# Clearing expert output columns later on GpSimd, and loading two float64 pieces later

## The chip, the cores and the metric

The kernel runs on one core of a Trainium2 chip. The metric is device microseconds of one execution; the kernel before takes 333.71 us, the median of three runs (333.45 to 333.76).

## The reference, cut to what matters

Three layers run one after the other on 1536 tokens of width 384.

```python
y = _attn_ref(r, k, v, w, u)                 # linear attention with a decaying state: 2 x 768 tokens, 8 heads of 48
logits = x @ w_gate                          # mixture of 8 experts, each token to its best one
# each expert takes its first `capacity` = 384 tokens; the others' output is zero
h = np.maximum(np.einsum('ecd,edf->ecf', disp, w1), 0.0)
out[i] = gate_w[i] * y[expert_idx[i], pos[i]]
h = x @ w_in; e = np.exp(h - h_max); sm = e / (e.sum() + 1e-9)      # SoLU block, w_in and w_out are float64
ln = (h * sm - mu) / np.sqrt(var + 1e-06) * g_ln
return (ln @ w_out).astype(np.float32)
```

## The kernel before, in words

**Attention** walks over 12 blocks of 128 tokens (`for m in range(NM - 1)`, then block 11 by itself). Each block ends as a tile of gated tokens that SP stores to DRAM (`store`, L481). GpSimd scatters the block's tokens' numbers into a table of slots (`scatter`, L486), SP loads a part of that table into `ids` (`load_ids`, L86), and GpSimd gathers an expert's tokens from DRAM with it, two indirect DMAs per expert (`load_xe`, L94). For expert 0 the tokens of the last blocks are not gathered but placed by matmuls with one-hot tiles (`add`, L654). Each of those needs a block's tokens split in a high and a low part; the low part of blocks 8 and 9 is a difference on GpSimd (L575), that of blocks 10 and 11 one on VectorE (L579).

**Experts.** One loop over g from 0 to 33 does a quarter of an expert's hidden layer per step, e being g // 4 and q being g % 4. `mm1(g)` (L822) makes a quarter of the hidden layer, ScalarE and VectorE evict it in a high and a low part (`hh` L828, `hl` L829), and `mm2(g - 2)` (L808 to L810) adds the quarter that was made two steps earlier into the output. The weights come as raw halves by SP (`load_half`, L107) and are split in high and low parts by ScalarE (L116) and VectorE (L122); in some steps GpSimd forms the low part with an adding DMA (L120). `xe_split` (L801 to L804) transposes the next expert's gathered tokens and splits them (`xlo`, L804). After the last quarter an expert's output is evicted to `yT` at a column known only at run time (L859 ScalarE, L860 VectorE); an expert writes 224 columns, of which the next expert's output overwrites the unused ones.

**Clearing.** `yT` is four tiles (high and low part, two shapes). At q == 0 of expert e GpSimd clears the 224 columns that start at (e + 1) * 224, in four memsets (L929), for e from 0 to 6. The first two sets of four run together, eight memsets behind the gather of expert 1.

**Pieces.** w_in and w_out are float64. Each comes as 8 pieces of 384 KB (`load_piece`, L140, on SP, three buffers) and is turned into high and low parts in the loop by ScalarE (L878, L879, L904) and VectorE (`decode_piece`, L887 to L906). Beside a piece's decoding runs one step of `later`, a chain of small VectorE operations on the experts' counts (`starts`, L738 to L754).

After the loop the SoLU block runs over 12 blocks of tokens, TensorE first (`h2`, L1016).

All engines take their instructions in the order in which the program gives them (the schedule is written by hand), and so does each queue: SP's holds the stores, table loads, pieces and raw halves, GpSimd's the scatters, gathers, adding DMAs, inverse positions (`inverse`, L787) and memsets.

Of the kernel before, what the change touches and what calls it, by code (L numbers as in the profile page):

```python
# [8 lines left out]
F32 = mybir.dt.float32  # L9
# [10 lines left out]
N, DM, NE, DF = B * S, H * D, 8, 1024  # L20
C = 128
NM = N // C
# [3 lines left out]
W = 224  # L26
# [9 lines left out]
def rwkv_moe_solu_kernel(  # L36
# [21 lines left out]
    YW = N + max(W, 128 * NOV)  # L58
# [10 lines left out]
    V, S, G, T = nc.vector, nc.scalar, nc.gpsimd, nc.tensor  # L69
# [18 lines left out]
    def load_xe(e, c0, nb, rows=N + 1, t=None):  # L88
        if t is None:
            t = xe_p.tile([128, nb, DM], F32, tag="xe", name=f"xe{e}_{c0}", bufs=1)  # L90
        for b in range(nb):
            c = c0 + b
            n = BW[c] if c < 2 else 128
            nc.gpsimd.indirect_dma_start(  # L94
                out=t[0:n, b, :], out_offset=None, in_=xs[0:rows, :],
                in_offset=bass.IndirectOffsetOnAxis(ap=ids[0:n, e, c:c + 1], axis=0), bounds_check=rows - 1, oob_is_err=False,
            )
        return t
# [37 lines left out]
    def load_piece(p, eng=nc.sync):  # L136
        t = w64_p.tile([128, 384, 2], I32, tag="w64", name=f"w64_{p}")
        s = (w_in if p < NP else w_out).rearrange("p a f -> p (a f)").bitcast(I32)
        j = p % NP
        eng.dma_start(out=t.rearrange("p n c -> p (n c)"), in_=s[:, j * 768:(j + 1) * 768])  # L140
        pieces[p] = t

    def attention(actx):
# [145 lines left out]
        def scores(m):  # L289
            A = a2.tile([128, 2, HP, C], F32, tag="A", name=f"A{m}")  # L290
            kt, rt = kts.pop(m), rts[m]
            both = ps_s.tile([128, 2, HP, C], F32, tag="s", name=f"sp{m}")
            sps = [both[:, r] for r in range(2)]
            for p in range(HP):
                for r in range(2):
                    ps = slice(64 * r, 64 * r + 64)
                    T.matmul(
                        sps[r][:, p], kt[ps, p, :], rt[ps, p, :], start=p == 0, stop=p == HP - 1, skip_group_check=True
                    )
            As[m] = (A, both)  # L300
# [12 lines left out]
        def values(m):  # L313
            yps = ypss[m] = [ps_y.tile([128, 2, C], F32, tag="y", name=f"yp{m}_{q}") for q in range(2)]
            for j in range(HP):
                va = vab[m % 3][:, j].rearrange("p b d -> p (b d)")[:, 0:112]
                T.matmul(
                    yps[j // 2][0:112, j % 2], va, ident, is_transpose=True, start=j % 2 == 0, stop=False,
                    skip_group_check=True,
                )  # L320
# [159 lines left out]
        def store(m):  # L480
            nc.sync.dma_start(out=xs[1 + m * C:1 + (m + 1) * C, :], in_=xgs[m])  # L481
# [3 lines left out]
        def scatter(m):  # L485
            ins = G.indirect_dma_start(  # L486
                out=idx[:, :], out_offset=bass.IndirectOffsetOnAxis(ap=slots.pop(m)[:, 0:1], axis=0),
                in_=row[:, m], in_offset=None, bounds_check=NX - 1, oob_is_err=False,
            )
            for other in scattered:  # L490
                tc.declare_no_dep(ins.ins, other.ins, reason="every token has its own slot")
            scattered.append(ins)
# [92 lines left out]
        for m in range(NM - 1):  # L585
            values(m)
            if m:
                if m + 1 < NM:
                    scores(m + 1)
                if m + 2 < NM:  # L590
                    prelude(m + 2)
                if m + 1 < NM:
                    mask_scores(m + 1)
            attend(m, lambda: ranks(m - 1) if m else None)
            if m == NM - 2:
                state(m)
            if m:
                together(gate2(m - 1))
            if m == NM - LAST + 1:
                xe0 = load_xe(0, 0, 2, 1 + (NM - LAST) * C, ld.tile([128, 3, DM], F32, tag="krv", name="xe0"))  # L600
            if m:
                scatter(m - 1)
            if m < NM - 2:
                state(m)
            while pend:
                pend.pop()()
            if m in first:
                pend.append(split_q(*first[m], False, defer=True))
            if m + 2 < NM:
                products = prelude2(m + 2)  # L610
                next(products)
            if m < NM - 2:
                decay(m + 1)
            tokens(m)
            if m + 2 < NM:
                together(gate1(m), products)
                weigh(m + 2)
                prelude3(m + 2)
            else:
                values(m + 1)  # L620
                attend(m + 1, lambda: None)
                together(gate1(m))
            if NM - LAST < m:
                if m < NM - 2:
                    onehots[m - 1] = place(m - 1)
                his[m - 1] = part(m - 1)
                los[m - 1] = other(m - 1, his[m - 1])
            chunks.pop(m)
            if m + 4 < NM:
                load_chunk(m + 4)  # L630
            if m:
                store(m - 1)
            if m in halves:
                load_half(*halves[m])
            if m == NM - LAST:
                load_ids(0, 1)
            if m == NM - 2:
                load_piece(0)


        m = NM - 1
# [27 lines left out]
        together(steps)  # L669
        scatter(m - 1)  # L670
        store(m - 1)
        load_piece(1)
        ranks(m)
        steps = gate2(m)
        next(steps), next(steps)
# [6 lines left out]
        whole(m)  # L682
        together(steps)
        store(m)
        scatter(m)
        load_ids(1, 2)
        spare(1, fill)
# [21 lines left out]
    def experts_and_solu():  # L709
# [9 lines left out]
        yT = [[ytp.tile([128, n, YW], F32R, name=f"yT{x}{n}") for n in (2, 1)] for x in ("hi", "lo")]  # L719
# [203 lines left out]
        load_half(1, 3)  # L923
        for g in range(NQ + 2):
            e, q = divmod(g, 4)
            if q == 0 and (e + 1) * W < YW:
                for n in range(2):
                    for x in range(2):
                        G.memset(yT[x][n][:, :, (e + 1) * W:min((e + 2) * W, YW)].bitcast(F32), 0.0)  # L929
            if g == 4:  # L930
                mm2(2)
                xe_split(1, xraw)
                xraw = load_xe(2, 0, 2)
                mm2(3)
            tokens = e and q == 2 and e + 1 < NE
            if g < NQ:
                mm1(g)
            if g == NQ + 1:
                mm2(NQ - 1, NQ - 2)
            elif g >= 2 and g not in (4, 5, NQ):  # L940
                mm2(g - 2)
            if g + 3 < NQ:
                split_q(1, g + 3, False)
            if g == 0:
                split_q(2, 2, False)
            if 2 <= g < NQ - 1:
                split_q(2, g + 1, g > 4 and g % 4 == 1)
            if tokens:
                xe_split(e + 1, xraw)
            if tokens and e + 2 < NE:  # L950
                xraw = load_xe(e + 2, 0, 2)
            if g % 2 and g // 2 + 2 < 2 * NP:
                load_piece(g // 2 + 2)
            if g % 2 == 0:
                j = g // 2
                if g and j + 3 < NQ // 2:
                    load_half(1, j + 3)
                if g and j + 2 < NQ // 2:
                    load_half(2, j + 2)
            if g == 0:  # L960
                load_ids(2, NE)
            if g in (8, 26):
                for _ in later:
                    pass
            if g == 16:
                later = positions()
            if NQ - 5 <= g < NQ - 1:
                for m in range(3 * (g - NQ + 5), 3 * (g - NQ + 6)):
                    inverse(m)
            if g == NQ - 2 and NOV:  # L970
                tc.no_sync_barrier()
                tc.mark_branch_hint_location("over", "LikelyTaken", [ENG.PE, ENG.Activation, ENG.DVE, ENG.Pool, ENG.SP])
            if g == 20 and NOV:
                most.append(nc.values_load(
                    mxi[0:1, 0:1], min_val=0, max_val=N, skip_runtime_bounds_check_because="a count of tokens",
                ))
            if dec:
                decode()
            if g % 2 and g < 4 * NP - 1:
                dec = decode_piece(g // 2)  # L980
                decode()
            if g % 2 == 0 and g // 2 < 2 * NP:
                decode_early(g // 2)
# [246 lines left out]
```

## Time and profile before

| | |
|---|---|
| runs | 333.71 us median (333.45 to 333.76) |
| profiled execution | 332.55 us, of which the span from first to last instruction is 330.8 us |
| TensorE busy | 315.5 us (95%) |
| VectorE busy | 242.7 us (73%) |
| ScalarE busy | 187.2 us (57%) |
| GpSimd busy | 148.0 us (45%) |

Attention takes about 76 us, the experts go on to about 212 us, and the SoLU block fills the rest. Busy shares are means over stages: what a change in one of them is worth is read from the waits in that stage. A timeline line has the start, the length, the engine, the line, the operation with its tiles and shapes, and, in brackets, how long the engine sat idle before it and what ended that.

### The profile page before, as it was taken

The page shows a single profiled execution, that of the slowest core. Times are in us where ns is not written, and L with a number is a line of the kernel's source. Part 1 is how long each engine was busy: PE and PEld are TensorE (multiplying, and loading weights), DVE is VectorE, ACT ScalarE, POOL GpSimd, SP SyncE. Part 2 cuts the span into 40 slices and gives each one's busy share as a digit, 9 for nine tenths or more (in the row PEclk, how much of TensorE's full clock was granted, in tenths as well). Part 3 has the DMA queues.
Part 4 walks back from the last instruction along what each step waited for, and adds up shares of the span by engine and source line. Part 5 has one row for each costly group of instructions (what it writes and reads, how often), then busy time and mean ns, then how long its engine had stood idle before and what let it go on. Part 6 is the DMA issues. An engine that isn't in the chain of part 4 may idle for free. (4 is left out here: it accounts for less than half of the span.)

```text
span 330.8 us, 7363 instructions
## 1 busy us (share of the span) xinstructions
PE 315.5 (95%) x2747; PEld 289.9 (88%) x2747; DVE 242.7 (73%) x557; ACT 187.2 (57%) x406; POOL 148.0 (45%) x197
## 2 busy tenths in 40 slices
PE   8899989999989999999999999999999999999990
PEld 3688868879979999999999999978999999999990
DVE  7899999958989999898999896258745555434310
ACT  2545645649549796969696966126454433444410
POOL 7989899572523241423232454414254222333321
PEclk9999999999999999999999999999999999999997
DMA  6999999353778998989898913100000000000010
GB/s 207 399 335 274 368 400 381 120 147 116 237 276 257 297 297 295 287 283 275 279 283 292 273 60 49 11 0 2 2 24 29 21 24 24 26 24 24 26 48 24
DMA packets 20394, 56.23 MB, mean 170 GB/s; under 512 B 6594, under 2 KB 9028, under 8 KB 20356
## 3 DMA queue, kind: packets, MB, share of 16 engines
q1 hardware_dynamic: 16916, 47.67, 41.0%
q0 software_dynamic: 3440, 8.06, 10.3%
q8 instruction: 22, 0.36, 0.4%
q14 instruction: 16, 0.13, 0.1%
HBM read 50.56 MB, written 5.16 MB: 168 GB/s over the span
## 5 line engine op out<-in xcount | busy, mean ns | idle before, releaser
L809 PE MATMUL yps<-hl,whi 128*128 128x224 f32 x192 | 52.9, 276 | 0.5 <-DVE hl L829 0.5
L122 DVE TENSOR_TENSOR wlo<-raw,whi 128x768 fp32r<-128x768 f32 x57 | 52.3, 952 | 1.2 <-ACT whi L116 0.9
L808 PE MATMUL yps<-hh,whi 128*128 128x224 f32 x192 | 52.7, 275 | 0.0
L810 PE MATMUL yps<-hh,wlo 128*128 128x224 f32 x192 | 52.5, 273 | 0.0
L116 ACT ACTIVATE whi<-raw 128x768 fp32r<-128x768 f32 x64 | 50.6, 840 | 0.3 <-ACT hh L828 0.3
L1050 POOL TENSOR_SCALAR e<-e,nmu 128x1024 f32<-128x1024 f32 x12 | 13.5, 1128 | 62.6 <-DVE nmu L1049 59.5
L1027 DVE TENSOR_REDUCE nm<-h 128x1 f32<-128x1024 f32 (+1 forms) x13 | 14.7, 1139 | 33.2 <-PE h L1016 30.0
L809 PEld LDWEIGHTS yps<-hl,whi 128*128 128x128 f32 x192 | 36.9, 192 | 0.7 <-DVE hl L829 0.7
L810 PEld LDWEIGHTS yps<-hh,wlo 128*128 128x128 f32 x192 | 36.9, 192 | 0.0
L808 PEld LDWEIGHTS yps<-hh,whi 128*128 128x128 f32 x192 | 36.9, 192 | 0.0
L120 POOL DMA_DIRECT2D wlo<-in_w x7 | 6.9, 986 | 66.2 <-ACT wlo L125 66.2
L1084 PE MATMUL o<-w_hi,shi 128*128 128x384 f32 x96 | 33.1, 345 | 0.0
L1085 PE MATMUL o<-w_lo,shi 128*128 128x384 f32 x96 | 32.2, 335 | 0.0
L1086 PE MATMUL o<-w_hi,slo 128*128 128x384 f32 x96 | 32.2, 335 | 0.0
L94 POOL DMA_INDIRECT xe<-xs,ids x16 | 20.3, 1270 | 20.6 <-PE xt L801 8.6
L822 PE MATMUL hps<-xlo,whi 128*128 128x224 f32 x192 | 26.8, 275 | 1.5 <-DVE xlo L804 1.5
L822 PE MATMUL hps<-xhi,whi 128*128 128x224 f32 x192 | 27.1, 277 | 0.1
L828 ACT ACTIVATE hh<-hps 128x448 fp32r<-128x448 f32 x32 | 17.4, 543 | 17.1 <-PE hps L822 16.5
L822 PE MATMUL hps<-xhi,wlo 128*128 128x224 f32 x192 | 26.6, 274 | 0.0
L822 PEld LDWEIGHTS hps<-xlo,whi 128*128 128x128 f32 x192 | 24.0, 192 | 1.7 <-DVE xlo L804 1.7
L822 PEld LDWEIGHTS hps<-xhi,whi 128*128 128x128 f32 x192 | 24.0, 192 | 0.6 <-ACT xhi L696 0.6
L822 PEld LDWEIGHTS hps<-xhi,wlo 128*128 128x128 f32 x192 | 24.0, 192 | 0.0
(186 smaller groups left out, 787.7 us busy)
## 6 DMA issues: line engine op xcount, KB each, us to landing
raw<-in_w SPq DMA_DIRECT2D x32, 768.0 KB, 7.2
krv<-in_krv SPq DMA_DIRECT2D x11, 576.0 KB, 6.8
rkT<-in_rkT SPq DMA_DIRECT2D x12, 512.0 KB, 7.6
w<-in_w_in SPq DMA_DIRECT2D x8, 384.0 KB, 5.2
w<-in_w_out SPq DMA_DIRECT2D x8, 384.0 KB, 5.6
wlo<-in_w POOLq DMA_DIRECT2D x7, 384.0 KB, 5.5
xs<-xg SPq DMA_DIRECT2D x12, 192.0 KB, 4.8
krv<-in_krv SPq DMA_DIRECT2D x1, 384.0 KB
```

Of the source, the lines that this page charges most:

```text
L94: nc.gpsimd.indirect_dma_start(out=t[0:n, b, :], out_offset=None, in_=xs[0:rows, :], in_offset=bass.IndirectOffsetOnAxis(ap=ids[0:n, e, c: ...
L116: S.activation(hi, raw, AF.Copy)
L122: V.tensor_tensor(lo, raw, hi.bitcast(F32), ALU.subtract)
L808: T.matmul(ps, w[0][ws], x[0][xsl], start=first, stop=False, skip_group_check=True)
L809: T.matmul(ps, w[0][ws], x[1][xsl], start=False, stop=False, skip_group_check=True)
L810: T.matmul(ps, w[1][ws], x[0][xsl], start=False, stop=last, skip_group_check=True)
L822: T.matmul(ps[:, f], w1s[g][i][:, kk, wf], x[j][:, kk], start=not (i or j or f or kk), stop=j == 1 and kk == KD - 1, skip_group_check=True,)
L828: S.activation(hh, ps, AF.Relu)
L1027: V.tensor_reduce(nms[j], ps, AX.X, ALU.max, negate=True)
L1084: T.matmul(ps, hi[:, f % 4], wo[0][:, f], start=f == 0, stop=False)
L1085: T.matmul(ps, hi[:, f % 4], wo[1][:, f], start=False, stop=False)
L1086: T.matmul(ps, lo[:, f % 4], wo[0][:, f], start=False, stop=f == KF - 1)
```

## The change

At attention's end, pieces 0 and 1 of w_in are loaded later: piece 0 after the store of block 10 instead of one block sooner, piece 1 after the store of block 11 instead of after that of block 10, and so in front of the table load for expert 1.

In the experts' loop the memsets at q == 0 go. Instead, at q == 2 of expert e (1 to 6), behind the issue of the gather for expert e + 2, GpSimd clears the 224 columns that start at e * 224, the ones in which expert e's output, three steps later, can land; the last set stops at column 1536. That makes 24 memsets in place of 28, and none in the first six steps of the loop.

```diff
--- before.py
+++ after.py
@@ -634,8 +634,6 @@
                 load_half(*halves[m])
             if m == NM - LAST:
                 load_ids(0, 1)
-            if m == NM - 2:
-                load_piece(0)
 
 
         m = NM - 1
@@ -669,7 +667,7 @@
         together(steps)
         scatter(m - 1)
         store(m - 1)
-        load_piece(1)
+        load_piece(0)
         ranks(m)
         steps = gate2(m)
         next(steps), next(steps)
@@ -682,6 +680,7 @@
         whole(m)
         together(steps)
         store(m)
+        load_piece(1)
         scatter(m)
         load_ids(1, 2)
         spare(1, fill)
@@ -923,10 +922,6 @@
         load_half(1, 3)
         for g in range(NQ + 2):
             e, q = divmod(g, 4)
-            if q == 0 and (e + 1) * W < YW:
-                for n in range(2):
-                    for x in range(2):
-                        G.memset(yT[x][n][:, :, (e + 1) * W:min((e + 2) * W, YW)].bitcast(F32), 0.0)
             if g == 4:
                 mm2(2)
                 xe_split(1, xraw)
@@ -949,6 +944,10 @@
                 xe_split(e + 1, xraw)
             if tokens and e + 2 < NE:
                 xraw = load_xe(e + 2, 0, 2)
+            if q == 2 and 0 < e < NE and e * W < N:
+                for n in range(2):
+                    for x in range(2):
+                        G.memset(yT[x][n][:, :, e * W:min((e + 1) * W, N)].bitcast(F32), 0.0)
             if g % 2 and g // 2 + 2 < 2 * NP:
                 load_piece(g // 2 + 2)
             if g % 2 == 0:
```

## Rows read from the trace of the kernel before

**Rows 1.** Busy time by stretch: length, PE, PEld, DVE, ACT, POOL, clock, DMA.

```profile
112.00:150.00 38.00, 38.00 (x344) 38.00 (x343) 35.06 (x60) 29.05 (x53) 10.19 (x14) 1.00 0.90 293
```

**Rows 2.** Waits of PE in the whole span: total, times, longest.

```profile
PE hps L822 <- DVE xlo L804: 1.5, 1, 1.5
...
PE x L661 <- DMA xe<-xs,ids: 0.6, 1, 0.6
...
PE yps L809 <- DVE hl L829: 0.5, 1, 0.5
```

**Rows 3.** Timeline of PE around the waits: start, length, line, operation.

```profile
88.38 0.27 PE L808 MATMUL yps<-hh,whi 128*128 128x224 f32 x1
...
89.13 0.37 PE L809 MATMUL yps<-hl,whi 128*128 128x224 f32 x1 [0.48 <-DVE hl L829]
...
91.12 0.74 PE L801 MATMUL xt<-ident,xe 128*128 128x128 f32 x6
...
93.73 0.83 PE L822 MATMUL hps<-xhi,whi 128*128 128x224 f32 x6
...
94.40 0.83 PE L822 MATMUL hps<-xhi,wlo 128*128 128x224 f32 x6
...
96.77 0.93 PE L822 MATMUL hps<-xlo,whi 128*128 128x224 f32 x6 [1.54 <-DVE xlo L804]
```

**Rows 4.** Timeline of DVE in the same stretch.

```profile
84.51 2.75 DVE L740 TENSOR_SCALAR cnt<-tot 128x8 f32<-128x8 f32 x1
...
88.46 0.61 DVE L829 SCALAR_TENSOR_TENSOR hl<-hps,hh 128x448 fp32r<-128x448 f32 x1
...
95.81 0.91 DVE L804 TENSOR_TENSOR xlo<-xt,xhi 128x384 fp32r<-128x384 f32 x2
```

**Rows 5.** Timeline of POOL: gather of expert 1, first and last of eight memsets.

```profile
81.81 1.37 POOL L94 DMA_INDIRECT xe<-xs,ids  x1 [5.48 <-DMA ids<-idx]
...
83.49 1.09 POOL L94 DMA_INDIRECT xe<-xs,ids  x1 [0.31 <-issue]
...
84.59 0.49 POOL L929 MEMSET yThi<- 128x448 f32 x1
...
86.92 0.30 POOL L929 MEMSET yTlo<- 128x224 f32 x1
```

**Rows 6.** Groups by shape on DVE: a tensor_scalar like L740, undisturbed.

```profile
L742 DVE TENSOR_SCALAR cnt<-cnt 128x8 f32<-128x8 f32 x1 | 0.2, 165 | 0.0
```

**Rows 7.** Timelines of POOL and DVE: a later burst's last memset, the decoding after it.

```profile
125.39 0.30 POOL L929 MEMSET yTlo<- 128x224 f32 x1
...
127.08 0.36 DVE L887 TENSOR_SCALAR da<-w 128x384 int32<-128x384 int32 x1
```

**Rows 8.** Timeline of POOL where the added memsets fall: the adding DMAs.

```profile
186.07 0.98 POOL L120 DMA_DIRECT2D wlo<-in_w  x1 [10.30 <-ACT wlo L125]
...
201.96 0.97 POOL L120 DMA_DIRECT2D wlo<-in_w  x1 [5.64 <-ACT wlo L125]
```

**Rows 9.** Timelines of POOL and PE at attention's end: block 9's difference, its matmuls.

```profile
70.76 1.04 POOL L575 TENSOR_TENSOR xl<-xg,xh 128x384 fp32r<-128x384 f32 x1
...
72.28 0.50 PE L654 MATMUL x<-P,xl 128*128 128x224 f32 x3
```

**Rows 10.** Timeline of SP at attention's end: DMA issues.

```profile
72.61 0.42 SPq L140 DMA_DIRECT2D w<-in_w_in  x1
...
75.35 0.32 SPq L481 DMA_DIRECT2D xs<-xg  x1
...
77.49 0.79 SPq L86 DMA_DIRECT2D ids<-idx  x2
```

**Rows 11.** The piece issued at 72.61, from issue to landing.

```profile
DMA to landing us min/median/max: 3.5/3.5/3.5
```

**Rows 12.** Timeline of ACT: the first reader of piece 0.

```profile
80.57 0.57 ACT L878 ACTIVATE w<-w 128x384 int32<-128x384 uint32 x1
```

**Rows 13.** The two gathers of expert 1, from issue to landing.

```profile
DMA to landing us min/median/max: 6.8/6.9/7.1
```


## The prediction

> **What bounds the kernel now.** I read the page first, then the busy time by stretch, the waits of each engine, and the timelines around the waits that were left. In the experts' loop TensorE never stops: from 112 to 150 us it is busy for 38.00 of 38.00, with VectorE next at 35.06 [rows 1]. So an edit there is worth only what it takes from or adds to TensorE's idle time, and the list of its waits is short: once 1.5 us for `xlo`, 0.6 for expert 0's gathered tokens, 0.5 for `hl` [rows 2]. The reader is to see that the first and the last lie within eight microseconds of each other, at 89.13 and 96.77 [rows 3], and that both are waits for VectorE.
>
> VectorE is late there because of one event. At 84.51 a tensor_scalar on 8 columns (L740) starts and takes 2.75 us, while its like (L742) takes 0.165 [rows 6]; it ends at 87.26 [rows 4]. On GpSimd the first of eight memsets starts at 84.59 and the last ends at 86.92 + 0.30 = 87.22 [rows 5]. A VectorE instruction was held for as long as GpSimd cleared columns, and everything behind it, `hl` at 88.46 and `xlo` at 95.81 [rows 4], came that much later.
>
> **The memsets.** Undisturbed, L740 would have ended at 84.51 + 0.165 = 84.68; it ended at 87.26, so VectorE lost 2.58 us. All eight memsets leave this place. What TensorE gets back is worked out from starts. A group of six matmuls of 224 columns takes 0.67 us, from 93.73 to 94.40, so one takes 0.11, and after 88.38 the next was due at 88.49 and came at 89.13: 0.64 lost. After the group at 94.40 the next was due at 95.07 and came at 96.77: 1.70 lost [rows 3]. Together 2.34; the waits that the profile itself puts down, 0.48 + 1.54 = 2.02, are the lower bound.
>
> Is all of it given back? With VectorE 2.58 earlier, `hl` ends at 88.46 + 0.61 - 2.58 = 86.49, two microseconds ahead of need. `xlo` is two instructions in a row that end near 96.72, and would end at 94.14; TensorE, itself 0.64 earlier, wants it at 95.07 - 0.64 = 94.43. That is 0.29 to spare, so nothing is late next on VectorE, and I take 2.34. If the slack were used up, the term shrinks by what is missing, not to nothing.
>
> Behind that point no engine has to give the time back: TensorE has no gap to swallow it [rows 1], weight loads are issued when VectorE frees their buffers, and so move with it.
>
> **The memsets that remain.** The sets for experts 1 to 5 stay where they run now. Today each set, though written two steps later, runs straight behind a gather, since GpSimd has nothing in between. They now must wait for the output of the expert before, which is written one step before the set in the program; behind a set that waits stand the next adding DMA and gather, which wait for ScalarE and TensorE anyway. The 24 waits I cost at nothing. One set is new at this place, that of expert 6, behind the adding DMA at 186.07. Eight memsets took 2.63 us [rows 5], so four take 1.3 (an estimate). Behind them stand twelve inverse scatters, the second half of which starts only after the DMA at 201.96, in front of which GpSimd idles 5.64 us [rows 8]; that idle time hides it. Nothing, then; at worst the 1.3 us falls on VectorE again.
>
> The Trainium skill's page "SBUF — State Buffer", section "SBUF: two separate sides", says that GpSimd and a VectorE instruction in a two-port mode exclude each other from a shared pair of ports, and that the second blocks until the first instruction is through. The trace agrees that VectorE is blocked; it differs on how long, since L740 waited for eight memsets and not for one. By the page's rule the memsets would account for one memset's length alone, which is a rival below.
>
> **The pieces.** Without piece 0 in the way, expert 0's second gather lands earlier, and TensorE's 0.6 us wait for it [rows 2] may go. What is late next is on GpSimd: the difference tile of block 9 is done at 70.76 + 1.04 = 71.80, and its matmuls start at 72.28 [rows 9]; with some 0.1 us from one to the other (an estimate: one matmul's step), 0.35 us can be gained. The ends are 0 (the gather is no earlier) and 0.6. The end of attention hangs on this chain of matmuls, so the 0.35 passes on to the start of the experts.
>
> Piece 0 now takes the place that piece 1 has at 72.61, where a piece lands 3.5 us after issue [rows 10, 11], at 76.1. Its first reader is ScalarE's L878 at 80.57 [rows 12]: 4 us later, so no cost. Piece 1 is issued behind the store at 75.35, so at 75.7, and lands near 79.2. The table load for expert 1 follows on SP at 77.49 [rows 10], when the piece still has up to 1.7 us to go. The gathers of expert 1 hang on that table: they start at 81.81 and 83.49 [rows 5], the second lands 6.8 to 7.1 later [rows 13], at 90.3 to 90.6, and its transposes are at 91.12 [rows 3]. The slack of 0.5 to 0.8 us is nearly eaten by the 0.64 that TensorE arrives earlier. So a delay of the table shows in full: the ends are 0 and 1.7 us. I take 0.4, nearer to the lower end: the table itself is under way from 77.49 until GpSimd stops waiting for it at 81.81 [rows 5], 4.3 us, and the piece is through in the first 1.7 of them.
>
> "DMA: Bandwidth & Descriptors", section "Queues, rings and completion order", in the Trainium skill, has the descriptors of one queue start in order; by it the table, behind piece 1 on SP's queue, would pay nearer to the whole 1.7. No row here shows such an order.
>
> **Sum.** -2.34 (VectorE released) - 0.35 (first gather) + 0.4 (table behind piece 1) = -2.3 us. From the profiled execution's 332.55 that is 330.25. The median of the runs, 333.71, lies 1.16 above the profiled execution; the change applies to either, so I predict 331.4.
>
> **Rivals.** *The second gather is late.* Piece 1 holds up the table for the whole 1.7 us, or the raw half that a freed VectorE lets SP issue sooner crowds the gather. Gain 2.34 + 0.35 - 1.7 = 1.0: 332.7. For it: the slack is gone. Against: the piece is through in the first 1.7 of the table's 4.3 us. Chance 0.13.
>
> *Only one memset counts.* L740 is held by the first memset alone, 0.49 us [rows 5], and the other 2.1 us have another cause, such as the gather in front, that stays. VectorE, and TensorE behind it, then gain 0.49; with 0.35 that is 0.8: 332.9. Against it: the hold ends within 0.04 us of the last memset. Chance 0.07. (It is what the rule of the page on SBUF would give.)
>
> *Slower: the later sets now hold VectorE.* Place: L887, a decoding tensor_scalar. A later set ends at 125.39 + 0.30 = 125.69 and L887 runs at 127.08, 1.39 us behind [rows 7]. If the sets slip against VectorE by more than that, because of their new waits, each can hold it for up to 1.3 us. In the first event TensorE paid 2.34 of 2.58, nine tenths; at that rate a set costs 1.2 us, so two of the five sets pay back the gain and three make it slower, by 3.6 - 2.3 = 1.3: 335.0. Against it: VectorE idles 2.94 of 38 us here [rows 1], which would swallow part, and the output waited for is written a step before a gather that itself waits for TensorE. Chance 0.06.
>
> **How the numbers follow.** The forecast has 0.74, with its own range from 330.5 (all bounds in favour: 2.34 + 0.6 = 2.9, and 0.3 of spread between runs) to 332.3 (2.02, nothing from the first gather, and 0.6 for the table: 1.4). The range 330.5 to 333.0 takes in the late gather and the one-memset case: about 0.85. 0.2% is 0.67 us, about what a measurement of this kernel can tell: faster is below 333.04. Forecast 0.74 plus most of the late gather, 0.08, plus 0.02 of the one-memset case give 0.84 faster; the rest of the two, 0.10, is no change; slower 0.06.
>
> **What would show it.** Right: L740 takes under 0.3 us, no PE wait for `hl` at step 4 or `xlo` of expert 1, PE's wait for the first gather gone, and every later mark (such as the adding DMA at 186.07) about 2.3 us sooner. Wrong: L740 still long with no memset beside it; a PE wait in front of the transposes (L801) for a DMA; L887 or another tensor_scalar over 1 us beside a memset.

## The result, and the profile after

The changed kernel takes 331.3 us (median of seven runs, 330.55 to 332.37) against 333.8 for the kernel before beside it (333.45 to 335.63): 0.9916 times, with a 95% interval of 0.9892 to 0.9939. The forecast was 331.4. The profiled execution took 331.4 us, span 329.6.

The waits of TensorE in the changed kernel (engine, tile, line, what was waited for, total, times, longest) no longer hold any of the three in [rows 2]:

```profile
PE xp L427 <- ACT ex L417: 1.6, 2, 1.2
PE sp L297 <- POOL kt L262: 1.6, 1, 1.6
PE wps L191 <- DVE warm L186: 1.3, 1, 1.3
PE h L1015 <- PEq L1171: 0.4, 1, 0.4
PE yp L330 <- DVE Sc L381: 0.4, 1, 0.4
PE yp L340 <- issue: 0.2, 1, 0.2
PE hps L821 <- issue: 0.2, 1, 0.2
```

None of those left lies between the first expert matmul and the experts' end. VectorE's timeline where it had been held [rows 4]:

```profile
85.26 0.17 DVE L737 TENSOR_SCALAR cnt<-tot 128x8 f32<-128x8 f32 x1
85.37 0.56 DVE L888 SCALAR_TENSOR_TENSOR da<-w,da 128x384 int32<-128x384 int32 x1
85.85 0.17 DVE L739 TENSOR_SCALAR cnt<-tot 128x8 f32<-128x8 f32 x1
...
87.11 0.62 DVE L828 SCALAR_TENSOR_TENSOR hl<-hps,hh 128x448 fp32r<-128x448 f32 x1
...
94.53 0.92 DVE L803 TENSOR_TENSOR xlo<-xt,xhi 128x384 fp32r<-128x384 f32 x2
```

L739 is the old L740: 0.17 us where it took 2.75. (Below, an instruction whose record lasts far longer than that of the same instruction alone is called held, and the extra time a hold.) `hl` starts at 87.11, `xlo` at 94.53. TensorE's timeline around the places that had waited [rows 3]; the row at 77.61 is the first expert matmul:

```profile
77.61 0.90 PE L821 MATMUL hps<-xhi,whi 128*128 128x224 f32 x6 [0.15 <-issue]
...
90.51 0.28 PE L808 MATMUL yps<-hl,whi 128*128 128x224 f32 x1
90.63 0.27 PE L809 MATMUL yps<-hh,wlo 128*128 128x224 f32 x1
...
91.75 0.74 PE L800 MATMUL xt<-ident,xe 128*128 128x128 f32 x6
...
95.02 0.83 PE L821 MATMUL hps<-xhi,wlo 128*128 128x224 f32 x6
95.69 0.83 PE L821 MATMUL hps<-xlo,whi 128*128 128x224 f32 x6
```

The reader is to see an unbroken step: 90.51 to 90.63 is one matmul, 95.02 to 95.69 a group of six. From the first expert matmul to the `xlo` group of expert 1 it is 95.69 - 77.61 = 18.08 us; in the kernel before it was 20.52 (from 76.25, the start of the same matmul there, to 96.77). That is 2.44 us less. From that group to the span's end it is 234.0 us in the kernel before (330.8 - 96.77) and 233.9 here (329.6 - 95.69), so nothing behind it gave the gain back. GpSimd's timeline [rows 5]:

```profile
76.50 0.97 POOL L486 DMA_INDIRECT idx<-row,slot  x1 [1.74 <-DVE slot L456]
82.84 1.70 POOL L94 DMA_INDIRECT xe<-xs,ids  x1 [5.37 <-DMA ids<-idx]
84.84 1.08 POOL L94 DMA_INDIRECT xe<-xs,ids  x1 [0.31 <-issue]
92.76 1.03 POOL L94 DMA_INDIRECT xe<-xs,ids  x1 [6.83 <-PE xt L800]
...
106.95 0.49 POOL L950 MEMSET yThi<- 128x448 f32 x1
```

Behind the gather at 84.84 comes no memset; the next thing is the gather for expert 2, and the first memset follows the gather of expert 3 at 106.95.

The two profiled spans differ by 1.2 us only, since in this profile the experts begin 1.36 us later than in the one before. About a microsecond of that arose in the blocks ahead of anything that the change moves: TensorE's `yp` matmuls (L340) that start at 58.11 in the kernel before start at 59.08 here. Block 11's `tokens` are then 1.88 us late (70.70 against 68.82), of which 0.5 is made up before the experts. A second profile of the same kernel (below) has `tokens` at 68.82 and the first expert matmul at 75.73, so the lateness is not a fixed part of the change; what makes attention's length vary is not known.

### The profile page after: what moved, and what is told of

It reads as the page before. It is cut to its first block, busy times and chain, and to the rows that moved or that the text cites. A ratio compares the mean times of both kernels' runs of the same rounds, so it can differ in the third digit from the quotient of the medians.

```text
span 329.6 us, 7363 instructions
## 1 busy us (share of the span) xinstructions
PE 315.8 (96%) x2747; PEld 290.0 (88%) x2747; DVE 240.8 (73%) x557; ACT 186.6 (57%) x406; POOL 146.8 (45%) x193
## 5 line engine op out<-in xcount | busy, mean ns | idle before, releaser
L122 DVE TENSOR_TENSOR wlo<-raw,whi 128x768 fp32r<-128x768 f32 x57 | 52.3, 951 | 1.2 <-ACT whi L116 0.9
```

What stands on the lines that cost most here:

```text
L122: V.tensor_tensor(lo, raw, hi.bitcast(F32), ALU.subtract)
```

## The experiments

Ten kernels ran, in three groups (four, four and two, in the order of the table). Each group has its own runs of the kernel before, on one chip (medians 333.62, 333.02 and 332.65 us), so times are compared within a group. Several times came in lower than expected, by up to 0.95 us: the expectations counted from the 333.8 and 331.3 of the first measurement, and the kernel before itself is 0.2 to 1.2 us below that in the groups. "To `xlo`" is TensorE's time from the first expert matmul to the `xlo` group of expert 1, read from each trace.

| kernel | us | ratio to before, 95% interval | to `xlo`, us |
|---|---|---|---|
| memsets only | 330.86 | 0.9909 (0.9889 to 0.9930) | 18.09 |
| pieces only | 333.01 | 0.9977 (0.9966 to 0.9988) | 20.52 |
| changed, eight memsets back | 333.27 | 0.9990 (0.9976 to 1.0004) | 20.51 |
| before, counts chain later | 331.50 | 0.9931 (0.9912 to 0.9950) | 18.09 |
| changed, again | 329.96 | 0.9925 (0.9901 to 0.9948) | 18.09 |
| memsets only, again | 330.26 | 0.9920 (0.9900 to 0.9940) | 18.09 |
| changed, four memsets back | 331.35 | 0.9952 (0.9936 to 0.9967) | 19.24 |
| changed, differences on VectorE | 330.32 | 0.9921 (0.9902 to 0.9940) | 18.08 |
| changed, no clearing | 329.95 | 0.9916 (0.9899 to 0.9934) | 18.09 |
| changed, sets three times | 330.29 | 0.9928 (0.9911 to 0.9946) | 18.09 |

**The two parts by themselves.**

```diff
--- changed kernel
+++ memsets only
                 load_ids(0, 1)
+            if m == NM - 2:
+                load_piece(0)
...
-        load_piece(0)
+        load_piece(1)
         ranks(m)
...
-        load_piece(1)
         scatter(m)
```

> The changed kernel with the two pieces loaded where the kernel before loads them, so the memsets' part of the change alone. Theory (the eight memsets behind expert 1's gather held VectorE): nearly the whole gain stays, 331.3 to 331.8 us; L739 takes 0.17 us and TensorE waits for neither hl nor xlo near 89 to 97. Rival (the gain is the pieces'): 333.5 us, as before.

The pieces alone are the same lines the other way round, applied to the kernel before.

> The kernel before with the two pieces loaded later, so the pieces' part alone. Theory: VectorE is still held for 2.6 us beside the memsets; only expert 0's first gather gains, 0.35 us: 333.2 to 333.9 us. Rival (the gain is the pieces'): 331.5 us. Second rival (the table behind piece 1 costs up to 1.7 us): TensorE waits in front of the transposes, 334.5 us or more.

The memsets alone have the whole gain, 18.09 us to `xlo`, no wait there. The pieces alone leave the hold as it was (VectorE's timeline):

```profile
85.44 2.75 DVE L739 TENSOR_SCALAR cnt<-tot 128x8 f32<-128x8 f32 x1
```

and still gain 0.1 to 0.3%. No profile of any kernel shows a TensorE wait in front of expert 1's transposes, so the second rival falls.

**The eight memsets put back.**

```diff
--- changed kernel
+++ eight memsets back
             e, q = divmod(g, 4)
+            if q == 0 and e < 2:
+                for n in range(2):
+                    for x in range(2):
+                        G.memset(yT[x][n][:, :, (e + 1) * W:min((e + 2) * W, YW)].bitcast(F32), 0.0)
```

> The changed kernel with the eight memsets put back behind the gather of expert 1 (those columns are then cleared twice). Theory: L739 is held again until the last of the eight ends, some 2.6 us, TensorE waits for hl and xlo again, and the time rises by 2.0 to 2.4 us over the changed kernel, to 333.3 to 333.9. Rival (one memset only, by the rule of the port lock): the hold is about 0.5 us and the time rises by 0.5, to 331.8. Rival (the gain comes from where the other memsets went): no change, 331.3.

The whole loss returns: 20.51 us, 333.27. VectorE's held row, and GpSimd's first and last memset:

```profile
85.18 2.76 DVE L739 TENSOR_SCALAR cnt<-tot 128x8 f32<-128x8 f32 x1
```

```profile
85.26 0.49 POOL L928 MEMSET yThi<- 128x448 f32 x1
...
87.59 0.30 POOL L928 MEMSET yTlo<- 128x224 f32 x1
```

The hold ends at 85.18 + 2.76 = 87.94, the memsets at 87.59 + 0.30 = 87.89. These memsets clear columns that are cleared again later, so nothing needs what they write: it is enough for the loss that they run in this place.

**The memsets left, the held operation moved.** This takes away the other half of the meeting.

```diff
--- kernel before
+++ counts chain later
             for stage in dec:
-                next(later, None)
+                if g > 1:
+                    next(later, None)
                 if stage:
```

> The kernel before, in which the chain of small tensor_scalar operations on the experts' counts (L738 to L744) no longer runs in step 1 but from step 2 on, so that beside the eight memsets VectorE has only operations with two tensor inputs (L889, L893), the uint16 operation L891 and evictions from PSUM. Theory A (a memset holds only a VectorE operation with one SBUF input, like tensor_scalar): no VectorE operation beside the memsets is longer than 1 us, TensorE's two waits go, 331.3 to 331.8 us with the memsets still there. Theory B (memsets hold any VectorE operation on SBUF): L889 or L891 is held for 2 us or more and the time stays, 333.5 to 334.

Theory A holds. The memsets run as before, and VectorE works through its operations beside them at full speed:

```profile
85.32 0.49 POOL L930 MEMSET yThi<- 128x448 f32 x1
...
87.66 0.30 POOL L930 MEMSET yTlo<- 128x224 f32 x1
```

```profile
84.77 0.56 DVE L889 SCALAR_TENSOR_TENSOR da<-w,da 128x384 int32<-128x384 int32 x1
85.36 0.56 DVE L891 CUSTOM_DVE_ANT_0 da<-w,da 128x768 uint16<-128x768 uint16 x1
85.95 0.56 DVE L893 SCALAR_TENSOR_TENSOR da<-mag,da 128x384 f32<-128x384 bf16 x1
86.43 0.62 DVE L829 SCALAR_TENSOR_TENSOR hl<-hps,hh 128x448 fp32r<-128x448 f32 x1
86.96 1.81 DVE L122 TENSOR_TENSOR wlo<-raw,whi 128x768 fp32r<-128x768 f32 x2
...
88.70 0.17 DVE L738 TENSOR_SCALAR cnt<-tot 128x8 f32<-128x8 f32 x1
```

L889, L893 and L122 have two tensor inputs from SBUF, L891 works on uint16, L829 reads PSUM: each takes what it takes anywhere (0.56, 1.81 for two of L122, and 0.61 to 0.62 us). L889 ends at 85.33, as the first memset begins, so it is the others that count. L738, moved, takes 0.17 at 88.70. So neither the memsets nor the place cost anything; their meeting with a tensor_scalar of this chain did. The 331.50 lies 0.64 above the memsets-only kernel although both take 18.09 us to `xlo`. From the `xlo` group to the span's end it takes 234.6 us in this kernel and 233.9 in the memsets-only one: at the start of the SoLU block TensorE waits 0.4 us for `yThi` (L859) in this kernel and in no other. Why was not followed.

**How long a hold lasts: four memsets in place of eight.**

```diff
--- changed kernel
+++ four memsets back
             e, q = divmod(g, 4)
+            if g == 0:
+                for n in range(2):
+                    for x in range(2):
+                        G.memset(yT[x][n][:, :, (e + 1) * W:min((e + 2) * W, YW)].bitcast(F32), 0.0)
```

> The changed kernel with four of the eight memsets put back behind the gather of expert 1. Theory (GpSimd keeps VectorE out until its whole run of instructions is through): L739 is held for some 1.3 us; VectorE has 0.25 us to spare at xlo of expert 1 (95.69 against 95.44 in the changed kernel's trace), so TensorE loses 1.05 and the time is 332.3 us. Rival (one instruction only, by the rule of the port lock): held 0.5 us, loses 0.25, 331.5 us.

```profile
84.78 1.47 DVE L739 TENSOR_SCALAR cnt<-tot 128x8 f32<-128x8 f32 x1
```

```profile
84.86 0.48 POOL L928 MEMSET yThi<- 128x448 f32 x1
...
85.91 0.30 POOL L928 MEMSET yTlo<- 128x224 f32 x1
```

Held to 86.25, the four memsets end at 86.21. TensorE lost 19.24 - 18.09 = 1.15 us (1.05 expected), and the time rose by 1.39 over the changed kernel of this group. The one-instruction rival falls: in the traces with four and with eight memsets, a run without a gap kept the tensor_scalar out to its end.

**A hold at another place: the sets three times.**

```diff
--- changed kernel
+++ sets three times
             if q == 2 and 0 < e < NE and e * W < N:
-                for n in range(2):
+                for _ in range(3):
+                  for n in range(2):
                     for x in range(2):
```

> The changed kernel with each set of four memsets issued three times, so that a set lasts some 3.9 us. In the trace of the changed kernel the decoding's tensor_scalar L886 starts 2.75 us after a set's beginning (124.04 against 121.29); now the set still runs then. Theory (any two-port operation that meets a run of memsets is held to the run's end): L886 takes some 1.0 to 1.5 us behind four or five of the six sets, where it took 0.36. Of these 4.5 us of holds TensorE loses between nothing (VectorE idles 8% of this stretch, 1.2 us per expert) and nine tenths, 4.0 us, as in the first event; I expect 1 us. Rival (the hold belongs to the first memsets' place alone): L886 stays at 0.36 us and the time stays.

GpSimd's first and last memset of one long set, and the decoding's tensor_scalar that now meets it:

```profile
121.62 0.49 POOL L951 MEMSET yThi<- 128x448 f32 x1
...
125.24 0.30 POOL L951 MEMSET yTlo<- 128x224 f32 x1
```

```profile
124.37 1.39 DVE L886 TENSOR_SCALAR da<-w 128x384 int32<-128x384 int32 x1
```

It takes 1.39 us and ends 0.2 behind the set's last memset (125.54). Behind four of the six sets L886 takes 1.09 to 1.39 us, behind one 0.51, where it takes 0.36 alone. Yet TensorE lost nothing. Busy time from 95 to 210 us (length, PE, PEld, DVE, ACT, POOL, clock, DMA share, GB/s) in the second profile of the changed kernel and with the long sets:

```profile
95.00:210.00 115.00, 115.00 (x1029) 114.78 (x1029) 101.59 (x183) 87.51 (x156) 42.01 (x53) 1.00 0.76 234
```

```profile
95.00:210.00 115.00, 115.00 (x1031) 114.82 (x1031) 104.92 (x183) 87.28 (x156) 57.31 (x101) 1.00 0.75 234
```

VectorE is busy 3.33 us longer and TensorE all 115.00 of 115.00 both times. The expected 1 us was too much. VectorE is idle for 13.41 of the 115 us in the changed kernel and for 10.08 with the long sets; that this idle time took up the holds is the likely reading, but it was not followed hold by hold.

**No clearing at all.** The edit removes the memsets at q == 2, so the unused columns are not set to zero.

> The changed kernel without any clearing of output columns (left out: the zeros that a dropped token's column would need). Theory (the sets that remain meet no two-port operation of VectorE and hide in GpSimd's idle time): no change against the changed kernel, within 0.3 us. Rival (the remaining 24 memsets still cost): 0.5 us or more faster.

329.95 us, 0.9916 of before, against 0.9925 and 0.9928 for the changed kernel and the long sets: no difference beyond the intervals. Within some 0.6 us (the half width of an interval), the 24 memsets that remain are free, the new set near the loop's end among them.

**The pieces once more, and attention's end.** The changed kernel and the memsets alone were run again beside each other.

> The changed kernel once more, beside the memsets alone on the same chip, and for a second profile of attention's end. All theories: 330.8 to 331.5 us. From TensorE's first expert matmul to the xlo group of expert 1: 18.1 us again, as in every run without a hold.

> The memsets' part alone again, beside the changed kernel. Theory (the pieces give 0.35 us at attention's end): 0.3 to 0.4 us slower than the changed kernel of this call. Rival (the pieces give nothing, since attention's end waits for other engines): equal within 0.3 us, or faster.

TensorE's timeline at attention's end, first of the changed kernel, then with the pieces as before; the first row is block 11's `tokens`, the last the first expert matmul:

```profile
68.82 1.04 PE L395 MATMUL xp<-sel,ys 112*128 112x104 f32 x8
...
69.78 0.79 PE L659 MATMUL x<-ident,xe 128*128 128x128 f32 x6
...
75.73 0.90 PE L821 MATMUL hps<-xhi,whi 128*128 128x224 f32 x6
```

```profile
68.89 1.04 PE L395 MATMUL xp<-sel,ys 112*128 112x104 f32 x8
...
70.78 0.69 PE L661 MATMUL x<-ident,xe 96*128 96x96 f32 x5 [0.62 <-DMA xe<-xs,ids]
...
76.30 0.90 PE L822 MATMUL hps<-xhi,whi 128*128 128x224 f32 x6
```

Without piece 0 in the way expert 0's second gather lands 3.9 us after its issue instead of 4.8, the wait for the gathered tokens is gone, and `tokens` to experts takes 6.91 instead of 7.41 us, 0.50 less. Not every trace shows this: with the pieces moved, 0.26 us of the wait is left in the kernel with four memsets back (landing 4.1 us after issue), and with the pieces unmoved there is no wait for the gather in the first memsets-only profile and in the one with the counts chain later, where `tokens` came over a microsecond later. By the medians the pieces give 0.30 us (329.96 and 330.26), by the ratios nothing (0.9925 and 0.9920), and the two ranges overlap, so the whole-time effect of the pieces is small and its size is not settled by them.

**The differences on VectorE.** In three traces of the first group (the expectation below counts four) a tensor_scalar at attention's end (L560) was held too, for 1.74, 1.80 and 1.01 us in all, as in the memsets-only kernel (VectorE, then GpSimd):

```profile
68.55 1.74 DVE L560 TENSOR_SCALAR P<-iota_w,t,rank_all 128x224 fp32r<-128x224 f32 x1
```

```profile
68.07 1.04 POOL L486 DMA_INDIRECT idx<-row,slot  x1 [0.30 <-DVE nmx L407]
69.15 1.00 POOL L575 TENSOR_TENSOR xl<-xg,xh 128x384 fp32r<-128x384 f32 x1
```

The hold ends 0.14 us behind L575 (70.29 and 70.15), but L575 alone does not account for it: L560 starts at 68.55, beside the issue of the scatter (L486), and alone would have ended at 68.94, ahead of L575's start. Whether the scatter's issue held it is open.

```diff
--- changed kernel
+++ differences on VectorE
             if i < NM - 2:
-                G.tensor_tensor(xl, xgs[i], xh.bitcast(F32), ALU.subtract)
+                V.tensor_tensor(xl, xgs[i], xh.bitcast(F32), ALU.subtract)
```

> The changed kernel with the low parts of blocks 8 and 9 (L575) formed by VectorE instead of GpSimd. In four of the profiles so far the tensor_scalar L560 at attention's end is held for 0.6 to 1.4 us and ends with GpSimd's L575. Theory (the same exclusion at a second place, on the way to the experts): L560 takes 0.4 us, the first expert matmul comes 0.5 to 1 us sooner, 330.3 to 330.8 us. Rival (attention's end hangs on something else): 331.3 us, or slower by the 1.1 us of work that VectorE takes over.

L560 then took 0.39 to 0.42 us, but the time was 330.32, no better than 329.96. This settles little, for the profile of the changed kernel in the same group has L560 unheld too (0.39 to 0.43 us). Where L560 had been held, ScalarE's eviction of block 11 (L346), ahead of the same matmuls, was late as well (69.82 in the memsets-only trace, with its input ready at 68.64). The hold is not what made it late: with the counts chain later, L346 starts at 69.56 with its input ready at 68.15, and L560 had taken 0.50. What did make it late stays open, as does why the profiles of the second and third group do not show it. So no version here beats the changed kernel by more than the intervals.

## Why the prediction was right

**VectorE released** (2.34 predicted). Right in mechanism, place and size: 20.52 to 18.08, 2.44 us. The spare time at `xlo` was put at 0.29 us; it is 95.69 - (94.53 + 0.92) = 0.24. No later engine gave the gain back: the 234.0 and 233.9 us above.

The rival in which one memset counts was wrong. The Trainium skill's page "SBUF — State Buffer", section "SBUF: two separate sides", bars a VectorE operation in a two-port mode while GpSimd holds the shared pair, and one with two SBUF inputs only if the GpSimd operation reads SBUF. On which operations are barred, the runs agree: with only two-input operations beside the memsets there was no hold (0.56 us for L893, 1.81 for two of L122). Whether the held tensor_scalars ran in a two-port mode no run shows. On the length they differ: it was 1.47 us for four memsets and 2.75 for eight, not one instruction's 0.49.

**The first gather** (0.35 predicted). Right in mechanism: the gather lands sooner and the wait of 0.6 us goes, in the pair of traces that starts alike. They give 0.50; the step that looked ahead to GpSimd's difference tile was a little too strict. The pieces-only kernel fits it (0.1 to 0.3% of 333.6 is 0.4 to 1.1 us). The two medians 0.30 apart do not tell it from nothing.

**The table behind piece 1** (0.4 predicted as a loss). This term was mis-sized: it is nothing. SP did issue the table's load later behind piece 1 (SP's timeline, the piece and then the load; before, the load was at 77.49 behind a store at 75.35 [rows 10]):

```profile
76.87 0.42 SPq L140 DMA_DIRECT2D w<-in_w_in  x1
80.39 0.79 SPq L86 DMA_DIRECT2D ids<-idx  x2
```

It waited there for the scatter's landing, 3.0 us against 1.7 in the memsets-only kernel of the second group. But the load itself then came back sooner: GpSimd's second gather starts 8.34 us after block 11's scatter here (76.50 to 84.84), 8.14 in the second profile, and 8.13 with piece 1 out of the way. Over all traces it is 8.12 to 8.42 us with piece 1 in front and 8.13 to 8.34 without, so 0.3 us at the very most and no clear difference. Against a slack that the prediction called nearly eaten no wait appeared. Why the load is quicker when it is later was not tried.

**The sum.** -2.34 - 0.35 + 0.4 was -2.3; measured by the traces -2.44 - 0.50 + 0 is -2.9. By the medians of the runs it is -2.5 in the first measurement (333.8 to 331.3) and -3.1 in the second group; by the ratios -2.8 (2.0 to 3.6) and -2.5 (1.7 to 3.3). The loss that was not there and two gains a little larger pull one way, by 0.65 us together, so the forecast gain lies at the small end of what was found. That the median came out at 331.3 against a forecast of 331.4 is therefore partly luck: the terms do not agree as closely as the total, and attention's length alone moved the start of the experts between 75.73 and 77.61 in two profiles of the same kernel. For the same reason one sign came out only roughly: the adding DMA of 186.07 is at 184.89 in the first profile of the changed kernel and at 183.02 in the second, 1.2 and 3.0 us sooner where 2.3 was expected. The chance of the range, about 0.85, is less than its parts add up to (0.74 + 0.13 + 0.07 = 0.94).

**The memsets that remain** (nothing predicted). Right: without them the time is the same. The rival in which later sets hold L887 needed a slip of 1.39 us. The long sets show its holds are real, but its price, nine tenths of each hold, was wrong there: TensorE lost nothing.

## What to carry to other kernels

A VectorE tensor_scalar of 8 columns that takes microseconds is worth looking up in GpSimd's timeline: if it ends with a run of GpSimd instructions, either of the two can be moved, and both moves gave the same gain to `xlo` here. What a hold costs has to be read from the engine behind it: a hold of 1.3 us (L739, four memsets) cost 1.15 where VectorE had 0.24 to spare, and four of 0.7 to 1.0 us (L886) cost nothing in a stretch in which VectorE was idle for 13.41 of 115 us. Loading something later on a shared queue is to be followed through to its last consumer, since a later issue (here 1.3 us of extra wait on SP) need not be a later arrival.

## What the runs showed of the hardware

The hold of a tensor_scalar lasted as long as GpSimd went from one memset to the next without a pause (1.47 us over four, 2.75 over eight), and one that arrived in the middle of a run waited for the rest of it (L886, 1.39 us).

Not every tensor_scalar is held. In the kernel before, beside GpSimd's tensor_tensor L575 (70.76 to 71.80 [rows 9]), one of a single column takes the 0.15 us that it takes elsewhere (VectorE's timeline):

```profile
71.14 0.15 DVE L453 TENSOR_SCALAR t<-rank_all 128x1 f32<-128x1 f32 x1
```

The held ones have 8 to 384 columns of 32 bits. What tells the two kinds apart was not tried.

While one was held, the records in front of it were stretched too, as in the kernel with the eight memsets back:

```profile
84.58 3.34 DVE L737 TENSOR_SCALAR cnt<-tot 128x8 f32<-128x8 f32 x1
84.70 3.23 DVE L888 SCALAR_TENSOR_TENSOR da<-w,da 128x384 int32<-128x384 int32 x1
```

Both end with L739, whose record starts at 85.18. In the kernel before, L738 and L889 in front of L740 have 3.34 and 3.22 us. They need not be holds of their own: in the changed kernel L737 runs beside the gather's issue (85.26, the gather from 84.84 to 85.92) in 0.17, and L893, the same operation as L888, takes 0.56 beside the memsets in the kernel with the counts chain later.
